# A gated linear attention and a hard-swish MLP on one core: the same steps in another order on every queue

## The chip, the cores and the metric

One Trainium2 chip, one of its cores. The time is the device time of one execution in microseconds (us); the figure that counts is the median of several runs.

## The reference

```python
def _attn_ref(q, k, v, alpha):            # batch 4, heads 8, seq 768, dim 48
    for t in range(S):
        state = alpha[:, :, t, :, None] * state + np.einsum('bhd,bhe->bhde', k[:, :, t], v[:, :, t])
        y[:, :, t] = np.einsum('bhd,bhde->bhe', q[:, :, t], state)
    return y

def _moe_ref(x, w_in, w_out):             # x: 3072 x 384, w_in: 384 x 2048, w_out: 2048 x 384
    h = x @ w_in
    relu6 = np.clip(h + 3.0, 0.0, 6.0)
    g = h * relu6 / 6.0
    return g @ w_out
```

The output y of the attention, with its heads side by side, is the x of the MLP. The state of a head is a 48 x 48 matrix that every token decays and adds to; it starts anew in each batch.

## The kernel before

**Staging.** The 3072 tokens are 24 chunks j of 128 (six to a batch). Attention works chunk by chunk, since the state goes from one to the next. Two chunks are a group g of 256 tokens (twelve groups), on which the MLP works. Both weight matrices stay in on-chip memory.

**A step.** The kernel is a list of short functions, its steps, and a string of about 1,800 words in `run` (L751 and after). A word such as `sc.6.1.2` calls one function with its numbers: here the scores of chunk 6, in the PSUM banks 1 and 2. Everything stands in `tc.manual_schedule()`: every engine, and SP's queue of transfers, executes its instructions in the order of the words, and waits in place if what it needs is not there. An instruction waits for what it reads, and for earlier readers of what it overwrites.

**Steps of attention** for chunk j (engine in brackets):

- `la`, `lk`, `lq`, `lv` [SP]: load alpha, k, q and v. `ta`, `tk`, `tq` put the time along the free axis: up to chunk 5 as transposes [PE, L282], from chunk 6 on as transposes of 32 x 32 blocks [DVE, L286] out of the tiles `quads`. These loads fill their tile but for two corners in each of the six tiles, which get 1.0 by a memset [POOL, L257] in `load_akq` when a tile is first used (chunks 6 and 7).
- `ca` places alpha [ACT L300, or DVE L286], `r` and `p` are the scans of the decay [DVE, L309 and L320], `k` and `q` scale by them [DVE, L332].
- `sc` scores [PE, L346], `m` mask [DVE, L356], `qa` a copy of q beside them [ACT, L366].
- `kb`, `ck` turn k by token [PE L374, ACT L378]; from chunk 8 on `kt`, `kw`, `kr` do it by DVE and by way of DRAM.
- `u` the chunk's two halves of k'v [PE, L429], `sm` the next state [DVE, L437 and L439], `st` its decay [POOL, L409], `sv` the copies of the state beside v [ACT; POOL in a batch's first half chunk].
- `ya`, `yb` the output [PE, L455], `cy` keeps it as x [ACT, L464].

**Steps of the weights.** The inputs are 64-bit floats. For each of 16 slices i: `w` loads it, `d1` (low word) and `d2` (magnitude) [ACT, L186 and L196], `dx` the sign [ACT, L191; slices 0, 1, 2, 4], `d3` clips and shifts [DVE: two instructions at L203 and L205 for those slices, three at L207, L208 and L210 for the others], `d4` adds the words as integers [POOL, L217].

**Steps of the MLP.** Groups 0 and 1 take the first product whole: `f` [PE, L478] or its halves `fa`, `fb` [L489], the gate `fr` [ACT, L494] and `fg` [DVE, L498]. From group 2 on a bilinear scheme of 20 block products replaces it: `M.g.i` [PE, L600], sums of x blocks `xc` and of weight blocks `y` [DVE, L537 to L541], `n` keeps a sum [ACT, L606], `o` adds up an output [DVE], `e` and `h` are its gate [ACT L494, DVE L498]. The second product of group 0 is `b` [PE, L516]; later groups use seven block products `P.g.i` [PE, L703] with sums `s` of g and `x` of w_out [DVE, L647 and L664], `K` [ACT], `G` [DVE or ACT] and the store `O` [SP]. `z` are matmuls that fill time.

**Memory.** The MLP has four PSUM banks, attention four others; `slots` and `raws` share the memory of g. Which bank or slot a step takes is the number in its word.

Of the kernel before, what the change touches and what calls it, by code (L numbers as in the profile page):

```python
# [17 lines left out]
def kernel(  # L18
# [32 lines left out]
    nc = tc.nc  # L51
    B, H, S, D = q.shape
# [8 lines left out]
    G = 2  # L61
# [185 lines left out]

    def load_akq(name, j):
# [6 lines left out]
        if j < FIRST + NQ:  # L255
            for o in (BLK, 3 * BLK):
                nc.gpsimd.memset(to[o : o + BLK, :, V - 1, D - BLK : BLK], 1.0)  # L257
# [463 lines left out]
    def store2(g, i):  # L721
# [8 lines left out]
        "lq": lambda j: load_akq("q", j), "lv": load_v, "w": load_weight,  # L730
# [202 lines left out]
```

## Time and profile before

| what | us |
|---|---|
| runs | 533.3, 533.65, 533.85 (median 533.65) |
| profiled execution, its time | 533.84 |
| its span | 531.8 |
| TensorE (PE) busy | 522.2 |
| VectorE (DVE) busy | 477.0 |
| ScalarE (ACT) busy | 257.4 |
| GpSimd (POOL) busy | 50.4 |
| one `M` (4 matmuls, 8 records in the trace, L600) | 0.89 |
| one `P` (8 matmuls, 16 records, L703) | 2.60 |
| one `f` (6 matmuls, 12 records, L478) | 2.69 |
| one L332, k for chunks 6 and later | 0.68 |
| one L207, median | 0.62 |
| one L217, the eleven of one kind | 1.61 |
| one pad memset, L257 | 0.14 to 0.24 |

The span is the time between the first and the last instruction of the profile; 2.04 us of the profiled execution lie outside it. A busy engine is one that executes; an idle one waits for a semaphore, for its own queue, or has nothing left. The profile gives, for each wait, what ended it, and for each group of instructions its idle time before. A figure such as L332 is the line of the kernel that issued the instruction.

### The profile page before, as it was taken

To read this page: it belongs to the slowest core of one execution; us is meant where nothing else is said; L and a number is where in the kernel's file an instruction comes from. 1 tells how busy PE (TensorE), PEld (TensorE's weight loads), DVE (VectorE), ACT (ScalarE), POOL (GpSimd) and SP (SyncE) were. 2 spreads that over 40 slices of the span, in tenths; PEclk is the share of its full clock that TensorE was granted. 3 is DMA by queue.
4 is the path that set the end of the run, shared out by engine and by line. 5 is a ranking of instruction groups with operands and counts; after the bars stand their busy time and mean duration, and the time that the engine had idled before them with its cause. 6 is when DMAs were issued, how large, how long until landed. Compare 5 with 4: busy or idle time off the path is not lost.

```text
span 531.8 us, 15143 instructions
## 1 busy us (share of the span) xinstructions
PE 522.2 (98%) x6306; PEld 496.9 (93%) x6306; DVE 477.0 (90%) x849; ACT 257.4 (48%) x503; POOL 50.4 (9%) x71
## 2 busy tenths in 40 slices
PE   7799999999999999999999999999999999999997
PEld 7698886789999999999999999999999999999997
DVE  6999989999999999999999999999999899496382
ACT  3889865212653553553544444642634544553340
POOL 5333425100000000000000000000000000000000
PEclk9999999999999999999999999999999999999999
DMA  9998887006615156254345356055364052100001
GB/s 173 218 254 247 211 231 156 18 2 149 155 31 118 30 125 139 49 137 100 89 107 118 90 123 143 18 134 111 92 138 105 10 110 44 44 2 2 15 16 37
DMA packets 124100, 54.40 MB, mean 102 GB/s; under 512 B 83328, under 2 KB 116864, under 8 KB 124032
## 3 DMA queue, kind: packets, MB, share of 16 engines
q1 hardware_dynamic: 124032, 53.44, 44.0%
q8 instruction: 49, 0.80, 0.7%
q14 instruction: 19, 0.16, 0.1%
HBM read 44.50 MB, written 8.91 MB: 100 GB/s over the span
## 4 chain that ended last, share of the span: by engine, by line
PE 81%; DVE 9%; ACT 3%; DMA 3%; POOL 2%; issue 1%; SPq 0%; DVEq 0%; POOLq 0%; ACTq 0%
PE m_ps L703 34%; PE m_ps L600 34%; PE m_ps L478 4%; PE t_ps L455 3%; PE t_ps L346 2%; PE t_ps L429 2%; DMA v<-in_v_dram 1%; DMA raw<-in_moe_w_out_dram 1%; DVE rings L647 1%; DVE R L309 1%; DVE raw L537 1%; ACT raw L186 1%; DVE g_sb L647 1%; ACT raw L191 1%; DVE w L537 1%
## 5 line engine op out<-in xcount | busy, mean ns | idle before, releaser
L606 ACT COPY g_sb<-m_ps 128x512 f32<-128x512 f32 x110 | 63.6, 584 | 123.7 <-PE m_ps L600 104.3
L703 PE MATMUL m_ps<-w,g_sb 128*128 128x192 f32 x704 | 121.7, 327 | 0.0
L703 PEld LDWEIGHTS m_ps<-w,g_sb 128*128 128x128 f32 x704 | 113.7, 190 | 0.4
L703 PE MATMUL m_ps<-rings,g_sb 128*128 128x192 f32 x528 | 91.5, 326 | 0.0
L703 PEld LDWEIGHTS m_ps<-rings,g_sb 128*128 128x128 f32 x528 | 85.4, 190 | 0.1
L600 PE MATMUL m_ps<-xc,w 128*128 128x128 f32 x640 | 82.8, 277 | 0.4 <-DVE w L541 0.4
L600 PEld LDWEIGHTS m_ps<-xc,w 128*128 128x128 f32 x640 | 77.5, 192 | 1.7 <-issue 0.6
L494 ACT ACTIVATE r<-g_sb,half 128x512 f32<-128x512 f32 x80 | 56.8, 722 | 33.1 <-DVE g_sb L541 12.1
L498 DVE SCALAR_TENSOR_TENSOR g_sb<-r,g_sb 128x512 f32<-128x512 f32 x80 | 53.7, 683 | 4.3 <-ACT r L494 3.9
L600 PE MATMUL m_ps<-xT,raw 128*128 128x128 f32 x400 | 52.5, 277 | 0.0
L600 PEld LDWEIGHTS m_ps<-xT,raw 128*128 128x128 f32 x400 | 48.6, 192 | 0.6
L409 POOL TENSOR_TENSOR st<-sm,R 128x192 f32<-128x192 f32 x20 | 12.9, 643 | 352.2 <-DVE sm L439 305.5
L647 DVE TENSOR_TENSOR g_sb<-g_sb 128x512 f32<-128x512 f32 (+1 forms) x55 | 41.9, 792 | 0.2
L600 PE MATMUL m_ps<-xT,w 128*128 128x128 f32 x320 | 42.0, 276 | 0.0
L600 PEld LDWEIGHTS m_ps<-xT,w 128*128 128x128 f32 x320 | 39.3, 192 | 0.1
L366 ACT COPY A<-q 48x256 f32<-48x256 f32 x88 | 35.6, 404 | 5.0 <-DVE q L332 3.8
L356 DVE TENSOR_TENSOR A<-t_ps,mask 64x256 f32<-64x256 f32 x96 | 36.0, 413 | 0.4
L478 PE MATMUL m_ps<-xT,w 128*128 128x256 f32 x144 | 32.8, 382 | 0.1
L600 PE MATMUL m_ps<-xc,raw 128*128 128x128 f32 x240 | 31.8, 276 | 0.0
L309 DVE TENSOR_TENSOR_SCAN R<-t,ones 128x516 f32<-128x516 f32 x24 | 29.6, 1235 | 1.0 <-ACT t L300 0.9
L478 PEld LDWEIGHTS m_ps<-xT,w 128*128 128x128 f32 x144 | 26.7, 190 | 3.8 <-POOL w L217 0.2
L600 PEld LDWEIGHTS m_ps<-xc,raw 128*128 128x128 f32 x240 | 29.6, 192 | 0.1
(104 smaller groups left out, 725.8 us busy)
## 6 DMA issues: line engine op xcount, KB each, us to landing
raw<-in_moe_w_out_dram SPq DMA_DIRECT2D x8, 768.0 KB, 5.3
raw<-in_moe_w_in_dram SPq DMA_DIRECT2D x6, 768.0 KB, 6.6
v<-in_v_dram SPq DMA_DIRECT2D x48, 96.0 KB, 3.1
out_dram<-oh SPq DMA_DIRECT2D x44, 96.0 KB, 1.7
far<-kq SPq DMA_DIRECT2D x64, 64.0 KB, 2.2
kb<-far SPq DMA_DIRECT2D x64, 64.0 KB, 2.1
aq<-in_alpha_dram SPq DMA_DIRECT2D x36, 96.0 KB, 2.7
qq<-in_q_dram SPq DMA_DIRECT2D x36, 96.0 KB, 2.5
```

The source lines that it names most:

```text
L309: nc.vector.tensor_tensor_scan(out=reverse(R, n - 1, n), data0=reverse(ax, n, n), data1=reverse(ones, n, n), initial=0.0, op0=ALU.mult, op ...
L356: nc.vector.tensor_tensor(out=to[:, a], in0=sc[a][half], in1=mask[half, half].unsqueeze(1).to_broadcast([HB, NP, HB]), op=ALU.mult)
L366: nc.scalar.copy(out=to[:, a], in_=Q_t[j][64 * a : 64 * a + D, :, half])
L409: nc.gpsimd.tensor_tensor(out=st, in0=sm, in1=R_t[j][:, :, 0:1].to_broadcast([C, NP, D]), op=ALU.mult)
L455: nc.tensor.matmul(y_of(j, (i + 1) // 2, p)[:, HB * b : HB * b + HB], vb[:, p, e : e + 32], A_t[j][:, b, 2 * p + a], start=(b == 0 and i = ...
L478: nc.tensor.matmul(h[:, f], w1[:, kk, o : o + C], xT_t[g][:, kk], start=(kk == 0), stop=(kk == KT - 1))
L494: nc.scalar.activation(out=to, in_=h, func=AF.Relu, bias=half, scale=1.0 / 6.0)
L498: nc.vector.scalar_tensor_tensor(out=to, in0=r, scalar=1.0, in1=h, op0=ALU.min, op1=ALU.mult)
L600: nc.tensor.matmul(acc[g][i][:, f * C : (f + 1) * C], spots[w][:, f * C : (f + 1) * C], x_of(g, x), start=(first and f == 0), stop=last, s ...
L606: nc.scalar.copy(out=slots[z], in_=acc[g][i])
L647: nc.vector.tensor_tensor(out=out, in0=in0, in1=in1, op=ALU.subtract)
L703: nc.tensor.matmul(to[g], a, rhs[:, f], start=(first and f == 0), stop=(last and f == HF - 1), skip_group_check=True)
```

## The change

The memsets of the corners leave `load_akq` and become a step of their own, `pd` (`pd.0` for the tiles of chunk 6, `pd.1` for those of chunk 7; six memsets each). All other words are the same, with the same banks and slots, in another order: on PE 345 of 436 steps have another place (2.4 places away in the mean, at most 17), on DVE 656 of 704 (6.7; at most 44), on ACT 353 of 414 (3.0), on POOL 26 of 46, on SP 162 of 190 (3.9).

The diff, with the first stage of the program (up to the first block products of group 2) and two later lines; the rest is of the same kind.

```diff
@@ -245,6 +245,11 @@
         b, c = divmod(j, NC)
         return t[b, :, c * C : (c + 1) * C, :]
 
+    def pad(r):
+        for name in "akq":
+            for o in (BLK, 3 * BLK):
+                nc.gpsimd.memset(quads[name, r][o : o + BLK, :, V - 1, D - BLK : BLK], 1.0)
+
     def load_akq(name, j):
         src = rows({"a": alpha, "k": k, "q": q}[name], j)
         if j < FIRST:
@@ -252,9 +257,6 @@
                               in_=src.rearrange("h s d -> s h d"))
             return
         to = quads[name, j % NQ]
-        if j < FIRST + NQ:
-            for o in (BLK, 3 * BLK):
-                nc.gpsimd.memset(to[o : o + BLK, :, V - 1, D - BLK : BLK], 1.0)
         to = to.rearrange("r p v d -> r p (v d)")
         t = src.rearrange("(p a) (u v) d -> a u p (v d)", a=2, v=V)
         for o in range(4):
@@ -727,7 +729,7 @@
 
     steps = {
         "la": lambda j: load_akq("a", j), "lk": lambda j: load_akq("k", j),
-        "lq": lambda j: load_akq("q", j), "lv": load_v, "w": load_weight,
+        "lq": lambda j: load_akq("q", j), "lv": load_v, "pd": pad, "w": load_weight,
         "d1": round_low, "d2": magnitude, "dx": sign, "d3": high_bits, "d4": add_low,
         "ta": lambda j, *i: transposed("a", j, *i), "tk": lambda j, *i: transposed("k", j, *i),
         "tq": lambda j, *i: transposed("q", j, *i), "ca": place_alpha, "r": decay, "p": growth,
@@ -748,156 +750,158 @@
             steps[name](*(int(x) for x in at))
 
     with tc.manual_schedule():
-        run("""z.0.5 z.0.3 z.0.1 z.0.8 qa.0.0 w.0 d2.0 d3.0 la.0 ta.0.0 ca.0 r.0 lk.0 tk.0.1 k.0
-               z.0.2 p.0 la.1 ta.1.2 lq.0 tq.0.3 ca.1 r.1 lk.1 lv.0.0 sv.0.0 d1.0 kb.0.0 ck.0 z.0.2
-               u.0.2.1 sm.0.0 sv.0.1 q.0 qa.0.1 tk.1.0 k.1 p.1 z.0.2 sc.0.2.3 m.0 la.2 ta.2.0 ca.2
-               dx.0 w.2 d2.2 kb.1.0 ck.1 lq.1 r.2 sm.0.1 st.1 tq.1.2 q.1 d3.2 z.0.3 d1.2 dx.2 lv.1.1
-               u.1.3.1 sv.1.0 sm.1.0 p.2 sm.1.1 sc.1.0.2 m.1 ya.0.3 yb.0 cy.0 lq.2 w.1 d1.1 tq.2.1
-               q.2 d4.2 lk.2 tk.2.3 k.2 fa.2.0 d4.0 st.2 sc.2.0.2 d2.1 d3.1 m.2 dx.1 d4.1 qa.1.1
-               lk.3 la.3 ta.3.1 ca.3 la.4 fa.0.1 sv.1.1 w.3 r.3 ta.4.3 ca.4 r.4 tk.3.1 k.3 kb.2.0
-               qa.1.0 d2.3 ya.1.2 yb.1 cy.1 fa.1.2 lq.3 ck.2 d1.3 p.3 d3.3 lv.2.2 u.2.3.2 sm.2.0
-               d4.3 fb.2 tq.3.1 q.3 fb.1 qa.2.0 sm.2.1 sv.2.0 st.3 fr.0.2.0 fg.0.2 lk.4 tk.4.0
-               sv.2.1 w.5 d2.5 k.4 d3.5 d1.5 qa.3.0 d4.5 qa.2.1 sc.3.1.3 m.3 w.6 d2.6 d1.6 d3.6 d4.6
-               lv.3.0 lq.4 w.7 kb.3.2 fb.0 f.0.3.3 kb.4.0 ya.2.1 ck.3 u.3.3.2 sm.3.0 fr.0.3.1 fg.0.3
-               fr.0.1.0 fg.0.1 qa.3.1 sv.3.0 sm.3.1 p.4 d2.7 sv.3.1 d1.7 d3.7 d4.7 f.0.5.0 fr.0.5.1
-               fr.0.0.0 fg.0.5 fg.0.0 tq.4.3 ck.4 la.5 ta.5.2 f.0.6.3 ca.5 w.4 d2.4 ya.3.0 yb.3 cy.3
-               fr.0.6.1 yb.2 cy.2 w.9 d2.9 q.4 qa.4.1 d1.4 d1.9 dx.4 la.6 w.8 d3.4 r.5 lk.5 w.10
-               d3.9 p.5 ca.6 fg.0.6 d4.9 w.12 lq.5 lv.4.1 d2.8 d3.8 f.0.7.2 d1.8 st.4 d4.8 d4.4 w.11
-               fr.0.7.0 fg.0.7 f.1.7.0 fr.1.7.1 fg.1.7 sc.4.0.2 m.4 f.1.1.1 fr.1.1.0 fg.1.1 f.1.3.3
-               fr.1.3.1 d2.10 d1.10 tk.5.3 f.1.0.2 d2.12 d3.10 d4.10 w.13 fg.1.3 fr.1.0.0 fg.1.0 k.5
-               d3.12 lq.6 f.1.6.0 f.1.2.1 u.4.1.0 sm.4.0 d1.12 d4.12 sv.4.0 qa.4.0 ya.4.2 fr.1.6.1
-               fg.1.6 w.15 tq.5.3 fa.4.3 sv.4.1 d2.11 kb.5.1 d2.13 fr.1.2.0 f.1.4.2 fr.1.4.1 d1.11
-               sm.4.1 q.5 r.6 d3.11 d3.13 fg.1.4 d4.11 lv.5.0 lk.6 tq.6 p.6 d2.15 d3.15 fg.1.2 d1.13
-               d4.13 sc.5.0.3 yb.4 f.1.5.0 fr.1.5.1 fg.1.5 tk.6 m.5 b.1.0.2 fb.4 b.1.1 d1.15 d4.15
-               st.5 y.5 w.14 la.7 lk.7 cy.4 d2.14 qa.5.1 ck.5 b.0.0.1 fr.0.4.0 d3.14 k.6 q.6 ca.7
-               fg.0.4 d1.14 d4.14 x.0 y.1 y.10 b.0.1 y.0 y.2 u.5.2 P.1.0.0 K.1.0 qa.5.0 sv.5.0
-               qa.6.1 P.1.1.3 b.0.2 b.1.2 kb.6.0 ya.5.3 y.6 s.1.0.0 sm.5.0 sv.5.1 G.1.0.0 tk.7
-               s.1.1.1 s.1.2.3 x.1 yb.5 cy.5 b.1.3 sc.6.1.2 lv.6.2 ck.6 u.6.3.0 s.1.3.2 x.2 P.1.2
-               b.0.3 K.1.1 y.7 s.1.4 s.1.5 y.11 y.3 r.7 xc.2.1 x.3 y.4 y.8 xc.2.3 k.7 xc.2.0 xc.2.4
-               y.9 y.12 y.16 y.13 y.15 P.1.3.3 K.1.2 P.1.4 bo.1 P.1.5 xc.2.5 G.1.1.1 P.1.6 y.14 y.17
-               y.19 xc.2.6 sm.6.0 G.1.2.2 y.20 M.2.0.2 lv.12.1 la.8 O.1.1 O.1.0 ca.8 y.18 y.21 y.23
-               so.1 G.1.3.3 n.2.0.8 bo.0 lq.7 lv.7.0 O.1.2 m.6 xc.2.2 xc.2.10 xc.2.7 tq.7 r.8 p.7
-               xc.2.8 sv.6.1 M.2.15.3 M.2.1 kb.7.3 n.2.1.9 M.2.16 M.2.2 n.2.2.10 M.2.7.0 n.2.7.11
...
-               xc.4.8 M.4.7.3 M.4.1 xc.4.2 h.3.2 o.3.7.1 lk.11 O.2.2 tk.11 e.3.6.0 e.3.3.1 h.3.3
-               P.3.1.2 e.3.7.1 n.4.1.13 M.4.2 K.3.0 ca.11 q.10 h.3.6 r.11 k.11 h.3.7 n.4.7.15
...
+        run("""z.0.5 z.0.3 z.0.1 z.0.8 qa.0.0 w.0 d2.0 d3.0 la.0 ta.0.0 ca.0 r.0 la.1 lk.0 ta.1.2
+               z.0.2 tk.0.1 k.0 ca.1 r.1 p.0 lv.0.0 lq.0 lk.1 d1.0 z.0.2 z.0.2 kb.0.0 tq.0.3 la.2
+               dx.0 ck.0 u.0.2.1 sm.0.0 sv.0.1 q.0 qa.0.1 tk.1.0 k.1 sc.0.2.3 ta.2.0 ca.2 w.2 d2.2
+               sm.0.1 m.0 r.2 p.1 d3.2 z.0.3 kb.1.0 ck.1 d1.2 lv.1.1 lq.1 tq.1.2 u.1.3.1 lk.2 w.1
+               lq.2 d4.0 st.1 sv.0.0 sv.1.0 dx.2 sm.1.0 q.1 p.2 sm.1.1 ya.0.3 yb.0 sc.1.0.2 m.1
+               cy.0 d1.1 tk.2.3 tq.2.1 k.2 q.2 st.2 d4.2 d2.1 d3.1 dx.1 d4.1 la.4 fa.0.1 ta.4.3
+               sc.2.0.2 fa.2.0 m.2 qa.1.0 sv.1.1 qa.1.1 lv.2.2 la.3 ta.3.1 ca.3 r.3 ca.4 r.4 kb.2.0
+               ya.1.2 yb.1 fa.1.2 ck.2 cy.1 p.3 u.2.3.2 sm.2.0 qa.2.0 lk.4 lk.3 w.3 tk.3.1 k.3 d2.3
+               d1.3 fb.2 fb.1 sm.2.1 d3.3 w.5 lq.3 tq.3.1 q.3 d1.5 sv.2.0 d2.5 fr.0.2.0 d3.5 qa.2.1
+               qa.3.0 w.6 fb.0 tk.4.0 sc.3.1.3 m.3 fg.0.2 kb.3.2 ck.3 qa.3.1 d2.6 d3.6 la.5 lv.3.0
+               lq.4 w.7 pd.0 d4.3 f.0.3.3 u.3.3.2 fr.0.3.1 sv.2.1 d1.6 la.6 w.4 pd.1 d4.5 st.3 d4.6
+               sm.3.0 k.4 sv.3.0 sm.3.1 fg.0.3 p.4 sv.3.1 fr.0.1.0 d2.7 d1.7 d3.7 d4.7 f.0.5.0
+               tq.4.3 kb.4.0 ck.4 fr.0.5.1 ta.5.2 f.0.6.3 ca.5 ya.3.0 yb.3 ya.2.1 cy.3 yb.2 q.4
+               fg.0.1 fg.0.5 w.8 r.5 lk.5 lv.4.1 lq.5 w.9 d2.8 d1.4 fr.0.0.0 fg.0.0 sc.4.0.2 m.4
+               d3.8 tk.5.3 f.0.7.2 k.5 qa.4.0 cy.2 fr.0.7.0 d1.8 d1.9 d2.9 fr.0.6.1 qa.4.1 d2.4
+               d4.8 st.4 fg.0.7 d3.9 fg.0.6 d3.4 d4.9 f.1.1.1 u.4.1.0 sm.4.0 tq.5.3 f.1.7.0 f.1.0.2
+               kb.5.1 f.1.3.3 lk.6 w.10 d2.10 fr.1.1.0 dx.4 fg.1.1 d3.10 p.5 fr.1.0.0 d1.10
+               fr.1.7.1 fg.1.7 d4.10 d4.4 fg.1.0 f.1.2.1 f.1.6.0 sv.4.1 f.1.4.2 sm.4.1 q.5 ca.6
+               tk.6 lk.7 ck.5 lv.6.2 w.12 w.11 d2.12 w.13 d1.12 fr.1.3.1 fg.1.3 d3.12 d4.12
+               fr.1.6.1 fg.1.6 fa.4.3 d2.11 sv.4.0 d1.11 d3.11 r.6 d4.11 lv.5.0 fb.4 ya.4.2 yb.4
+               sc.5.0.3 la.7 w.15 w.14 ca.7 qa.5.0 d2.13 d1.13 fr.1.4.1 fg.1.4 cy.4 fr.1.2.0 d2.15
+               d1.15 d2.14 qa.5.1 k.6 d3.13 m.5 d3.15 p.6 fg.1.2 d3.14 d1.14 fr.0.4.0 u.5.2 f.1.5.0
+               fr.1.5.1 b.1.0.2 kb.6.0 b.1.1 b.0.0.1 b.0.1 ck.6 sv.6.0 d4.13 st.5 d4.15 d4.14 y.6
+               fg.1.5 P.1.0.0 la.9 lq.6 tq.6 sm.5.0 sv.5.1 sv.5.0 K.1.0 ya.5.3 yb.5 cy.5 y.3 r.7
+               fg.0.4 x.0 q.6 y.5 s.1.1.1 s.1.0.0 sc.6.1.2 u.6.3.0 b.1.2 P.1.1.3 b.1.3 b.0.2 bo.1
+               so.1 xc.2.2 y.1 s.1.3.2 s.1.2.3 y.7 x.1 y.10 xc.2.1 x.2 sm.6.0 tk.7 xc.2.3 y.11 y.0
+               G.1.0.0 y.9 s.1.5 xc.2.4 y.2 y.8 y.4 k.7 P.1.3.3 P.1.2 K.1.2 qa.6.1 K.1.1 P.1.5
+               xc.2.5 xc.2.0 y.13 y.16 s.1.4 y.15 y.12 y.17 xc.2.6 xc.2.7 y.19 y.20 x.3 y.18 sv.6.1
+               kb.7.3 P.1.4 G.1.1.1 M.2.0.2 b.0.3 P.1.6 sm.6.1 xc.2.8 y.21 xc.2.9 st.7 lq.8 lq.7
+               lv.7.0 lv.12.1 la.8 lk.8 tq.8 y.23 tq.7 y.14 ca.8 p.7 ck.7 n.2.0.8 bo.0 G.1.3.3
+               M.2.1 n.2.1.9 M.2.7.0 M.2.2 n.2.7.11 n.2.2.10 M.2.8 M.2.3 z.1.3 M.2.4 n.2.4.12 ca.9
...
+               o.3.7.0 p.10 o.3.7.1 tk.11 tq.10 h.3.2 e.3.6.0 n.4.0.10 M.4.1 M.4.7.3 K.3.0 n.4.1.13
+               M.4.2 h.3.6 n.4.7.15 e.3.3.1 n.4.2.14 M.4.8 xc.4.9 q.10 h.3.3 P.3.1.2 e.3.7.1 M.4.3
...
```

## The prediction

> **What bounds the kernel now.** I read the page first: busy time, then the slices.
>
> ```profile
> PE 522.2 (98%) x6306; PEld 496.9 (93%) x6306; DVE 477.0 (90%) x849; ACT 257.4 (48%) x503; POOL 50.4 (9%) x71
> ...
> PE   7799999999999999999999999999999999999997
> ...
> DVE  6999989999999999999999999999999899496382
> ...
> PEclk9999999999999999999999999999999999999999
> ```
>
> TensorE (PE) is busy 522.2 of 531.8 us at an undiminished clock, so an order can only regain its 9.6 us of gaps or the price of switching between kinds of matmul. VectorE (DVE) at 90% is the second bound, and the stretches (PE, PEld, DVE, ACT, POOL busy; clock; DMA) say where:
>
> ```profile
> 0.00:20.00 20.00, 15.45 (x152) 13.61 (x152) 14.99 (x30) 10.00 (x15) 7.12 (x20) 1.00 1.16 204
> 20.00:40.00 20.00, 18.30 (x395) 16.56 (x396) 19.64 (x34) 18.44 (x30) 8.84 (x7) 1.00 1.05 227
> ...
> 100.00:130.00 30.00, 29.58 (x278) 24.80 (x277) 29.84 (x53) 5.26 (x13) 0.00 (x0) 1.00 0.20 48
> 130.00:170.00 40.00, 40.00 (x538) 38.87 (x537) 39.38 (x71) 20.14 (x40) 1.60 (x2) 1.00 0.46 104
> ...
> 450.00:490.00 40.00, 40.00 (x454) 39.50 (x453) 28.45 (x56) 17.25 (x35) 0.00 (x0) 1.00 0.08 20
> ```
>
> PE idles up to 31 us and a little before 130; later it never waits. DVE is full from 20 to 170 us (29.84 of 30.00 in 100:130) and has room only near the end. So up to about 140 us the two are bound together: what delays DVE there must reach PE as soon as the spare of some pair "DVE writes, PE reads" is used up. What waits there, for DVE from 6 to 110 us:
>
> ```profile
> DVE w L203 <- ACT w L196: 2.5, 1, 2.5
> DVE s L439 <- PE t_ps L429: 1.1, 1, 1.1
> DVE R L309 <- ACT t L300: 0.9, 1, 0.9
> DVE s L437 <- PE t_ps L429: 0.2, 1, 0.2
> ```
>
> The first lies at its start; the second is sm.4.0 waiting for u.4. Last the chain of waits in the steady part:
>
> ```profile
> 183.88 1.92 PE t_ps L455 x128
> 185.81 1.98 PE m_ps L600 x16
> 187.79 2.60 PE m_ps L703 x16
> ...
> 193.89 1.78 PE m_ps L600 x16
> ```
>
> It is PE alone. Two M products cost 1.78 us, but 1.98 behind attention's small matmuls: a visit to the small ones costs some 0.3 us beside its own work (0.1 ahead of it, 0.2 behind).
>
> **The sum, part by part.** It is made against the profiled execution: span 531.8 and 2.04 outside it, 533.84 us, 0.19 above the median of 533.65. Work is the same on every engine, so only order counts. On PE 345 of 436 steps move, by 2.4 places in the mean; on DVE 656 of 704, by 6.7.
>
> *Pads.* Twelve POOL memsets of 0.14 to 0.24 us, 2.3 us in all, become pd.0 and pd.1, ahead of d4.3 and d4.5. POOL is 91% idle and has no transfer behind it: I take nothing. If POOL were late there, 1.2 us (one pd) would be added to a conversion; if they now leave the loads of chunks 6 and 7 earlier, up to 0.3 us is gained.
>
> *Fewer switches.* Between big products and small attention matmuls PE goes 50 times in the old order and 45 in the new. Counted over the words with the prices above, the steady part saves 0.84 us. The old 0.42 us that M.2.0 waits for xc at 127.5 us is also in reach. Together -1.26; bounds 0 and -1.3.
>
> *DVE work ahead of what PE needs.* For a pair I take the old spare (end of the writer to start of the reader), less DVE work newly put ahead, plus PE work newly put ahead of the reader, less PE work no longer there.
>
> - q.6 (ends 94.64) to sc.6 (starts 108.85): spare 14.21. DVE does ca.7, y.6, sm.5.0, y.3, r.7, fg.0.4, x.0 first (6.23 us) and y.5 later (0.61); PE no longer does P.1.1, b.0.2, b.1.2, b.1.3 first (10.34 us). 14.21 - 6.23 + 0.61 - 10.34 = -1.75.
> - G.1.0 (102.19) to P.1.3 (115.12): 12.93 - 10.08 + 0.60 - 5.18 = -1.73.
> - q.7 (134.63) to sc.7 (140.31): 5.68 - 2.83 + 1.30 - 5.35 = -1.20.
>
> ```profile
> 108.85 0.69 PE L346 MATMUL t_ps<-q,k 48*64 48x64 f32 x32
> ...
> 140.31 0.69 PE L346 MATMUL t_ps<-q,k 48*64 48x64 f32 x32
> ```
>
> These are one lateness seen three times, not a sum: +1.75 us of PE waiting, unless DVE arrives earlier than before. Others stay near nothing (fg.1.2 to b.0.0 about -0.55), and later single pairs go to -1.25 (h.3.3 to P.3.1), the same lateness again.
>
> *DVE waits that go and come.* The 1.14 us at sm.4.0 go: u.4 now stands ahead of two f products of 2.69 us on PE. New, placed by hand from the rows of each step: 0.15 at sm.0.0 (dx.0, 1.9 us on ACT, is put ahead of ck.0, and u.0 needs ck.0), 0.25 at r.3 (for ca.3, on ACT behind the copies qa and sv), 0.4 at d3.7 (d2.7 stands behind sv and d1.6 on ACT), 0.75 at fg.0.0 (fr.0.0 stands behind d2.8, which waits for w.8): +1.55, bounds 0 and 2.2. SP's queue moves too: lq.3 goes behind w.3 and w.5 and lands near 36.1 instead of 31.75, w.9 behind w.8, lk.5, lv.4, lq.5 near 57.4 instead of 51.35; behind each on its engine (DVE's q.3; ACT's d2.9, fr.0.6, qa.4.1) stands work that I find covered by other DVE work; bounds 0 and 1. In the steady part every load leads its reader by 2 us or more: nothing.
>
> *DVE beside POOL.* Some DVE operations stand still while POOL adds integers (d4, L217):
>
> ```profile
> 92.40 1.69 POOL L217 TENSOR_TENSOR w<-raw 128x768 int32<-128x768 int32 x1 [3.73 <-DVE raw L210]
> ```
>
> ```profile
> 92.69 1.96 DVE L332 TENSOR_TENSOR q<-q,P 128x512 f32<-128x512 f32 x1
> ...
> 133.95 0.68 DVE L332 TENSOR_TENSOR q<-q,P 128x512 f32<-128x512 f32 x1
> ```
>
> q.6 took 1.96 instead of 0.68 and ended within 0.6 us of POOL's end; d3.15's L207 took 1.77 instead of 0.62 beside another d4. [...] By position, the new order puts d4.3 beside d3.5 (0.8), d4.8 beside d3.9 (0.3), d4.9 beside d3.4, d4.12 beside d3.11 and d4.15 beside d3.14 (0.9 each), and takes away the two shown (1.28 and 1.15): 3.8 - 2.43 = +1.37. Start times differ by some tenths from my placing, and a hold is there or not by such tenths: bounds -2.4 (none of the new) and +3.8 (the old two replaced by equal ones). I take +0.9, two thirds of the count.
>
> Sum: +1.75 - 1.14 + 1.55 + 0.9 - 1.26 = +1.80 us: 533.84 + 1.80 = 535.64 for a profiled execution, 535.45 for the median.
>
> **Rivals.** *PE alone decides (faster).* Place: sc.6, sc.7 and P.1.3. If none of the new holds comes while both old ones go (-2.4) and half of the waits come (+0.8), DVE's lateness is 1.75 - 1.14 + 0.8 - 2.4 = -1.0: it is early, PE keeps the -1.26 and gets up to 1.0 us of its idle time before 31 us, since DVE then no longer takes it back. 533.65 - 1.26 to -2.26 is 531.4 to 532.4; I put 532.0. It decides once lateness is below nothing. For it: PE's visits are fewer throughout, and u.4 and the f products are better interleaved. Against: DVE is full in 100:130, and three pairs independently come out negative.
>
> *Nothing is seen.* Neither new waits nor holds count: 1.75 - 1.14 - 1.26 = -0.65, 533.0; with the waits alone +0.9, 534.55. For it: my waits of 0.15 to 0.75 us are near the error of the placing. Against: all have the same sign.
>
> *DVE falls further behind (much slower).* Every counted hold comes and the old are only replaced: 1.75 - 1.14 + 1.55 + 3.8 - 1.26 = +4.7, 538.35. For it: DVE has no idle time there to absorb one. Against: in the whole old run the holds sum to some 5 us, and POOL's work is the same.
>
> **How the numbers follow.** A measurement of this kernel can tell 0.2%, 1.07 us, from no change. The sum passes +1.07 once new waits and holds together exceed 1.72 us; I estimate 2.45, with bounds of -2.4 and 6. The forecast gets 0.42, much slower 0.08, so slower 0.50; nothing seen 0.23; PE alone 0.27, the most I can give it with DVE as full as it is. Predicted 535.4. The range goes from the first rival's 532.0 to 538.0, short of the last rival's end. The forecast's own range is 534.7 to 537.
>
> **What would show it.** Right: PE waits for L332 or L286 of DVE at sc.6 or sc.7 (L346), 1 to 3 us in all, between 95 and 145 us; the 1.1 us wait of L439 gone; several L207/L208 of 1.5 us or more beside L217; PE busy from 150 us on without waits and its steady part shorter by 0.5 to 1 us, with fewer "L600 x16" of 1.98. Wrong, faster: no PE wait after 31 us, DVE idle about 1 us somewhere in 100:140. Wrong otherwise: a DMA as releaser of PE in 30:70 (lq.3, w.9), or new PE waits after 150 us, where I count none, which would say that my spares in the steady part are too large.

## The result, and the profile after

Slower: a median of 541.77 us (540.45 to 543.38) beside 533.75 us (533.3 to 534.06) of the kernel before, a ratio of 1.0152 [1.0122, 1.0183]. The side was foretold, the size was not: +8.0 us instead of +1.8, above the range. The profiled execution took 543.38 us; its span is 541.6 us, 9.8 us longer than before. In the kernel after, lines have moved: L429 is L431, L439 is L441, L455 is L457, L498 is L500, L516 is L518, L600 is L602, L606 is L608, L703 is L705.

From the page of the kernel after, the parts that answer to those shown of before:

```profile
PE 525.8 (97%) x6306; PEld 499.7 (92%) x6306; DVE 478.2 (88%) x849; ACT 258.8 (48%) x503; POOL 53.3 (10%) x71
...
PE   8798899899999999999999999999999999999997
...
DVE  6899799999999999999999999999999996377381
...
PEclk9799899999999999999999999999999999999999
```

Two things differ. PE is busy 3.56 us longer with as many instructions, and idle 6.24 us longer (12.99 against 6.75 from the start of the span to its last instruction). And PEclk has a 7 and an 8 where before had only nines. The stretches of the kernel after (PE, PEld, DVE, ACT, POOL busy; granted clock; DMA) place both:

```profile
0.00:20.00 20.00, 14.47 (x151) 12.76 (x152) 15.48 (x30) 12.20 (x18) 10.09 (x22) 0.97 1.12 185
20.00:40.00 20.00, 19.38 (x379) 17.79 (x381) 17.01 (x30) 15.95 (x27) 5.89 (x10) 0.86 1.11 241
...
100.00:130.00 30.00, 29.24 (x269) 24.48 (x268) 29.93 (x48) 6.00 (x15) 0.44 (x1) 1.00 0.30 69
130.00:170.00 40.00, 39.52 (x532) 38.14 (x531) 39.55 (x76) 20.35 (x40) 1.63 (x2) 1.00 0.39 89
```

In 20:40 PE is busy for 19.38 us instead of 18.30 and still finishes 16 instructions fewer: the clock was 0.86. DVE lost 2.6 us there. Its full stretch, 100:130, is as full as before (29.93), and PE now waits in it. PE's waits in the kernel after, grouped (total, times, longest):

```profile
PE t_ps L284 <- DVE P L322: 2.4, 1, 2.4
PE t_ps L457 <- issue: 2.1, 1, 2.1
PE t_ps L348 <- DVE q L334: 1.7, 3, 0.8
...
PE m_ps L518 <- DVE g_sb L500: 1.1, 1, 1.1
PE t_ps L431 <- ACT r L496: 0.9, 1, 0.9
PE m_ps L602 <- issue: 0.7, 1, 0.7
PE m_ps L705 <- issue: 0.7, 1, 0.7
```

The third and fourth rows hold what was foretold. The first is tq.1, at 17.06 to 19.49 us. The row names p.1 on DVE, which ended at 19.39; but tq.1 does not read what p.1 writes, it reads the load lq.1, which landed at 19.35. The fifth is u.3, which overwrites the bank that m.3 reads. The three "issue" rows are waits in which the trace shows no data that was missing.

Put together, with the place of each item in the trace:

| what | us |
|---|---|
| 10.24 us at half clock (18.95 to 25.78 and 56.50 to 59.91): the same instructions take about 2.2 and 1.6 us longer than at full clock | +3.8 |
| "issue" stops: 2.06 in yb.2 (53.57), 0.66 at P.4.4 (271.12), 0.68 in M.8.13 (389.20) | +3.4 |
| waits for DVE: 1.11 at b.0.0 (94.83), 0.76 at sc.6 (105.00), 0.48 at sc.7 (141.53) | +2.35 |
| u.3 waits for m.3 (43.59) | +0.86 |
| the old wait at M.2.1 is gone | -0.42 |
| some 25 more products that take 0.05 us longer, most of them behind a copy (below) | +1.25 |
| what remains; five fewer visits to the small matmuls at 0.3 us would be that | -1.5 |
| sum | +9.74 |

The profiled execution is the slowest of the four. A second profile of the same kernel (the run "again" below) is 6.3 us longer than before instead of 9.8: its stop in yb.2 is 0.42 us, that in P.4.4 0.40, and the second half clock is missing.

PE's idle time ahead of 31 us is the same in both kernels, about 6.2 us; only its pieces differ. Behind PE's first instruction none is over 0.95 us before, and one is 2.43 after. The findings are taken in turn.

### The profile page after: what moved, and what is told of

Same layout as the page of the kernel before. It is cut to its first block, busy times and chain, and to the rows that moved or that the text cites. A ratio compares the mean times of both kernels' runs of the same rounds, so it can differ in the third digit from the quotient of the medians.

```text
span 541.6 us, 15103 instructions
## 1 busy us (share of the span) xinstructions
PE 525.8 (97%) x6306; PEld 499.7 (92%) x6306; DVE 478.2 (88%) x849; ACT 258.8 (48%) x503; POOL 53.3 (10%) x71
## 4 chain that ended last, share of the span: by engine, by line
PE 76%; DVE 14%; DMA 4%; issue 2%; SPq 2%; POOL 1%; ACT 1%; DVEq 0%; POOLq 0%
PE m_ps L705 34%; PE m_ps L602 33%; PE t_ps L457 4%; PE t_ps L348 2%; PE t_ps L431 2%; DMA raw<-in_moe_w_out_dram 2%; DMA raw<-in_moe_w_in_dram 1%; PE m_ps L491 1%; SPq L256 1%; DVE g_sb L500 1%; DVE w L207 1%; DVE raw L210 1%; DMA rings<-in_q_dram 1%; PE t_ps L284 1%; DVE P L322 1%
## 5 line engine op out<-in xcount | busy, mean ns | idle before, releaser
L705 PE MATMUL m_ps<-w,g_sb 128*128 128x192 f32 x704 | 122.2, 327 | 0.0
L608 ACT COPY g_sb<-m_ps 128x512 f32<-128x512 f32 x110 | 63.9, 584 | 112.2 <-PE m_ps L602 81.5
L705 PEld LDWEIGHTS m_ps<-w,g_sb 128*128 128x128 f32 x704 | 113.8, 190 | 1.3 <-DVE oh L721 0.5
L705 PE MATMUL m_ps<-rings,g_sb 128*128 128x192 f32 x528 | 91.8, 327 | 0.7 <-issue 0.7
L705 PEld LDWEIGHTS m_ps<-rings,g_sb 128*128 128x128 f32 x528 | 85.4, 190 | 1.3 <-issue 0.8
L602 PE MATMUL m_ps<-xc,w 128*128 128x128 f32 x640 | 82.8, 277 | 0.0
L602 PEld LDWEIGHTS m_ps<-xc,w 128*128 128x128 f32 x640 | 78.0, 192 | 0.8
L500 DVE SCALAR_TENSOR_TENSOR g_sb<-r,g_sb 128x512 f32<-128x512 f32 x80 | 53.8, 684 | 8.4 <-ACT r L496 4.4
L602 PE MATMUL m_ps<-xT,raw 128*128 128x128 f32 x400 | 52.2, 277 | 0.0
L411 POOL TENSOR_TENSOR st<-sm,R 128x192 f32<-128x192 f32 x20 | 14.4, 720 | 350.4 <-DVE sm L441 251.9
L602 PEld LDWEIGHTS m_ps<-xT,raw 128*128 128x128 f32 x400 | 48.5, 192 | 0.3
L602 PE MATMUL m_ps<-xT,w 128*128 128x128 f32 x320 | 42.5, 277 | 0.0
L602 PEld LDWEIGHTS m_ps<-xT,w 128*128 128x128 f32 x320 | 39.1, 192 | 0.3
L539 DVE TENSOR_TENSOR g_sb<-g_sb 128x512 f32<-128x512 f32 x40 | 27.0, 682 | 11.7 <-ACT g_sb L608 11.5
L602 PE MATMUL m_ps<-xc,raw 128*128 128x128 f32 x240 | 32.6, 278 | 0.7 <-issue 0.7
L602 PEld LDWEIGHTS m_ps<-xc,raw 128*128 128x128 f32 x240 | 29.7, 191 | 1.2 <-issue 0.9
```

What stands on the lines that cost most here:

```text
L411: nc.gpsimd.tensor_tensor(out=st, in0=sm, in1=R_t[j][:, :, 0:1].to_broadcast([C, NP, D]), op=ALU.mult)
L500: nc.vector.scalar_tensor_tensor(out=to, in0=r, scalar=1.0, in1=h, op0=ALU.min, op1=ALU.mult)
L539: eng.tensor_tensor(out=out, in0=in0, in1=in1, op=ALU.add if s1 > 0 else ALU.subtract)
L602: nc.tensor.matmul(acc[g][i][:, f * C : (f + 1) * C], spots[w][:, f * C : (f + 1) * C], x_of(g, x), start=(first and f == 0), stop=last, s ...
L608: nc.scalar.copy(out=slots[z], in_=acc[g][i])
L705: nc.tensor.matmul(to[g], a, rhs[:, f], start=(first and f == 0), stop=(last and f == HF - 1), skip_group_check=True)
```

## The experiments

Every kernel ran beside the kernel before, whose medians were 533.46 to 533.72 us. "Old" and "new" are the orders of before and after. Where the words of one order are followed by those of the other, each step is taken once, and the place of the change can have waits of its own; they are named.

### Where the time is lost: parts of the program

**old40**

```diff
- all words in the new order
+ old order up to f.0.3, the rest in the new order
```

> The old order up to f.0.3 (about 41 us, 152 words), then the new order of everything else. Theory A: no half clock before 31 us; the loads after 41 us are still in the new order, so the stop of 2 us at yb.2 (an instruction block fetched late behind those loads) may remain; median 535 to 538. Rival C (the new order pays at the pairs of DVE and PE between 95 and 145 us and in the steady part, whatever the opening does): 539 or more.

538.44 us, 1.0093 [1.0078, 1.0108]. The clock was 1.00 throughout, and tq.1's long wait and the stop in yb.2 were gone. At the cut u.3 still waited 0.61 us, for the copy ck.3 now, and tk.5 waited 0.74 us for its load. The waits for DVE stayed (1.15, 0.77, 0.45), and so did two stops (0.66 and 0.41). So the first 40 us are worth some 3 us, and more than half of the loss lies behind them.

**old128**

```diff
- all words in the new order
+ old order up to M.2.0, the rest in the new order
```

> The old order up to M.2.0 (about 128 us), then the new order of everything else. Theory A: only the two stops of 0.66 and 0.68 us for instructions and about 0.5 us at sc.7 remain, less up to 0.8 us of fewer switches: 534 to 535.5. Rival C: most of the 8 us remains, 538 or more.

538.17 us, 1.009 [1.0073, 1.0107], some 3 us above what was expected. The cut made a wait of its own (1.73 us at M.2.1, for y.23), and sc.7 waited 1.02; but the part behind M.5 took 2.0 us longer than in before, and no recorded wait explains it. So the new order of the steady part costs time inside PE's busy time. In the trace of old128, 25 products behind M.5 take some 0.05 us more each (1.3 us together; in before none does), and P.4.4 and M.8.13, where the kernel after has its stops, take 0.35 and 0.16 us more. The 0.05 us are what the copies, below, are about.

**new40 and mid**

```diff
- all words in the old order
+ new40: new order up to f.0.3, the rest in the old order
+ mid: old order up to f.0.3, new order up to M.3.0, the rest in the old order
```

> The new order up to f.0.3 (about 41 us), then the old order of everything else. Theory A (the 8.2 us are three separate parts that add up: the opening, the DVE pairs between 85 and 145 us, and the steady part): the opening's share, that is the idle lump with its half clock, 2 to 3.5 us: 536.5 (535.6 to 537.1), in executions whose mean clock is below 1.00. Rival C (a late opening costs nothing by itself, since DVE and PE catch up before 100 us): 533.6 to 534.4.

> Old order up to f.0.3, new order from there to M.3.0 (about 155 us), old order after it. Theory A: PE waits for DVE at b.0 (1.1), sc.6 (0.8) and sc.7 (0.5), together 2.4 us, less the 0.4 of the old order at M.2.1: 535.6 (535.0 to 536.5), clock 1.00. Rival E (the loss lies in the opening and in the steady part alone): within 0.5 us of the kernel before.

new40 took 541.55 us, 1.0142 [1.0123, 1.0161], 5 us more than expected. Its cut delays k.4, so that PE waits 4.31 us at 44.37 for it, and the clock is halved a second time. It says nothing of the order, but from M.5.0 to the start of P.11.6 it takes 292.85 us, exactly as before. mid took 537.37 us, 1.0067 [1.0053, 1.0082], 0.9 above the upper end expected. Its waits for DVE are 1.14, 0.77 and 0.47; 0.88 at the cut, 0.62 for a load (tk.5), 0.37 at u.2 and 0.29 at kb.5 come on top.

**old155**

```diff
- all words in the new order
+ old order up to M.3.0, the rest in the new order
```

> Old order up to M.3.0 (about 155 us), new order after it. Theory F (in the steady part a product that goes on in a PSUM bank waits until ACT has copied the partial sum out, the n step; a P between the two covers the copy, one M covers all but 0.05 us, nothing leaves 0.67 us): the steady part has 31 places with one M between instead of 7, so 24 x 0.05 = 1.2 us; with up to 1.3 us of stops for instruction blocks near 267 and 385 us 534.8 to 536.2. Theory D (the 0.05 us come from DVE being late): 533.6 to 534.2, since DVE starts this part on time.

539.16 us, 1.0101 [1.0086, 1.0115]; expected was 534.8 to 536.2. Waits at the cut (1.17, 0.35, 0.56) and a stop of 0.44 are one part, and 1.8 us of PE's steps from M.5.0 on, inside its busy time as in old128, the other.

**part1, part2 and part3**

```diff
- all words in the old order
+ part1: the first 125 words (37 us) new, the rest old
+ part2: 125 words old, then new up to word 661 (192 us), the rest old
+ part3: 661 words old, the rest new
```

> New order for the first 125 words (to about 37 us), old order after; at this cut the two orders have done the same steps but two. Theory A: the idle lump at tq.1 with the half clock behind it, 535.6 (534.6 to 536.6), in executions with a mean clock below 1.00; no PE wait after 45 us that the kernel before has not. Rival C (the opening's loss is caught up before 100 us): within 0.6 us of the kernel before.

> Old order for the first 125 words, new order to word 661 (about 37 to 192 us), old order after. Theory A: PE waits for DVE at b.0, sc.6 and sc.7, 2.4 us together, 0.4 less at M.2.1, 0.3 us of products with one M beside a copy; with the clock at 1.00: 536.0 (535.2 to 537.2); the stop at yb.2 should be small, since the loads before it are on time. Rival E: within 0.6 us of the kernel before.

> Old order for the first 661 words (to about 192 us), new order after. Theory F: from 230 us to the end 294.4 us instead of 292.85 without stops for instruction blocks, up to 1.3 more with them; one product at the cut (M.4.2) has nothing between it and the copy, 0.67 us: 536.2 (535.4 to 537.6). Parts 1, 2 and 3 together less 0.7 are then about the 8.2 us of the whole change. Rival D: 533.6 to 534.8.

part1: 535.56 us, 1.0031 [1.0019, 1.0043], as expected. It is 2.2 us late at 45 us and stays so to the end: PE is busy 1.4 us longer, at the halved clock (19.61 to 26.44), and idle 0.8 us longer, where sc.3 waits 1.15 us for DVE at the cut. part2: 537.43 us, 1.0073 [1.0048, 1.0098], 1.4 above its middle; waits of 1.46, 0.76 and 0.45 and a stop of 1.75 in yb.2, which had been expected to be small behind the old opening. part3: 539.27 us, 1.0104 [1.0089, 1.0119], 3 us above; cut waits 1.6, a stop of 0.78, and 1.9 of PE's steps. The three differences are 1.84, 3.71 and 5.55 us; less some 2 us that the cuts make, the sum is about 9.1, where the whole change costs 6.5 (the run "again", below) to 8.0 us. They don't add exactly; each part nonetheless costs time by itself.

### The clock: one long wait instead of several short ones

TensorE's granted clock is halved in stretches of 3.41 us or 6.83 us, on a grid of 3.413 us that runs through the whole execution (in the kernel after the clock changes at 18.95, 25.78, 56.50, 59.91 and, behind PE's last instruction, 541.19 us, which lie 2, 9, 1 and 141 such steps apart; it is 0.50 in 18.95:25.78 and in 56.50:59.91). The same step at both clocks, PE's timeline of the kernel before and after:

```profile
22.16 1.10 PE L455 MATMUL t_ps<-A,v 128*32 128x64 f32 x64 [0.92 <-DVE s L439]
```

```profile
22.02 1.93 PE L457 MATMUL t_ps<-A,v 128*32 128x64 f32 x64 [0.62 <-DVE s L441]
```

**nofill** takes four steps of fillers out of the old order, so that its idle time gathers in one place, a lump.

```diff
- p.0 behind z.0.2; u.0.2.1 behind z.0.2; sc.0.2.3 behind z.0.2; d1.2 behind z.0.3
+ the same without these four fillers
```

> The kernel before without nine filler matmuls (z.0.2 four times, z.0.3 once, about 2.5 us of PE between 8 and 18 us, all in places where PE then waits anyway). Theory A (what closes the clock is the share of idle time within a stretch of 3.4 us): PE idles more than 1.4 of 3.4 us somewhere between 10 and 22 us, the clock goes to half for one or two stretches, and the time rises by 1 to 3 us, to 534.5 to 536.5, although work is left out. Rival B: the work removed lay in idle time, no change, 533.0 to 533.7.

534.34 us, 1.0014 [1.0005, 1.0023]. PE was idle for 1.62 us in one piece, and the clock was halved, in the timed executions too. The stretch from 19.5 to 26.3 us, of before and then of this kernel:

```profile
19.50:26.30 6.80, 4.83 (x148) 4.23 (x148) 6.71 (x15) 6.68 (x9) 3.98 (x3) 1.00 0.93 185
```

```profile
19.50:26.30 6.80, 6.36 (x140) 5.95 (x141) 6.27 (x13) 6.00 (x9) 4.14 (x3) 0.50 0.99 192
```

Nearly the same instructions (140 against 148) fill 6.36 us instead of 4.83. The cost is only 0.7 us, less than the 1 to 3 us expected, since PE had 1.97 us to spare in that stretch of before. So the clock is closed by the lump, not by the new order as such, and what it costs hangs on PE's slack there.

**lq1** brings tq.1's load forward, **fill** puts a filler into the lump.

```diff
- d1.2 lv.1.1 lq.1 tq.1.2
+ lq1:  d1.2 lq.1 lv.1.1 tq.1.2
+ fill: d1.2 lv.1.1 lq.1 z.0.8 tq.1.2
```

> The changed kernel with one word moved: lq.1 is loaded ahead of lv.1.1 instead of behind it. Theory A (PE's idle time in one lump halves its clock for whole stretches of 3.4 us, and PE and DVE then pass the loss on): tq.1 starts near 17.8 us instead of 19.5, the wait of 2.43 us breaks into pieces of at most 1.3 us, the granted clock stays 1.00 between 15 and 30 us, and the median falls from 541.8 to about 539.3 (538.5 to 540.3). Rival B (the half clock is only a sign; what counts are the waits, and their sum in the opening is unchanged): the sum of PE's waits before 31 us stays near 5 us and the median falls by less than 0.6 us.

> The changed kernel with eight more filler matmuls (z.0.8, about 2.2 us) in the place where PE waited 2.43 us for tq.1; no step moves and no load is earlier. Theory A: the same data arrive at the same time, but the clock stays 1.00 from 15 to 30 us; and as the 32 more instructions move the limits of PE's instruction blocks (256 instructions each), the stops of 0.66 and 0.68 us near 270 and 389 us go: median 538.8 (537.8 to 539.8). Rival B: filler changes nothing, 541.2 to 541.8.

lq1: 540.34 us, 1.0137 [1.0114, 1.0159]. tq.1 waited 0.43 us instead of 2.43, which shows that the load was what it waited for; but u.1 then waited 1.87 us for lv.1, and the clock was halved from 19.15 to 25.98 as before. The lump had only moved. fill: 540.23 us (536.76 to 541.3), 1.0116 [1.0082, 1.015], above the range expected. Here the clock stayed full to 53 us, as expected; then a stop of 2.48 us in yb.2 halved it from 53.33 to 60.16. The one execution at a mean clock of 1.000 took 536.76 us, those at .994 to .997 took 540.2 to 541.3.

Over all profiles that show a change of the clock, and so the grid, taking PE's idle time inside one stretch of it in the first 150 us: each stretch with at least 1.77 us of it was followed by half clock. Of the stretches at full clock with 1.38 us or less none was (over 30 had between 0.9 and 1.38; the largest of before, behind PE's first instruction, is 1.20). Between these the outcome varied: 1.39 closed it once, 1.46 and 1.51 did not. It is the sum within a stretch that counts, not one long wait: in best and part3 (their openings are the old one) a wait of 0.95 us and one of 0.8 to 0.9 fell into one stretch, 1.77 and 1.83 us, and the clock was halved for 3.41 us.

The half clock also spreads the times of the kernel after: 543.38 us at a mean clock of .990, 542.31 and 541.24 at .994, 540.45 at .997.

### The stops without missing data: blocks of PE's instructions

**again** is the kernel after, unchanged, profiled a second time.

```diff
  no change to the kernel after
```

> The changed kernel once more, for its profile. Theory A: PE stops again at the same places of its instruction stream (before the 1474th, 6594th and 9666th PE record: yb.2, P.4.4 and M.8.13), each until 1.3 to 1.5 us after the landing of the 16 KB block; the clock closes where PE idled more than about 1.7 us of a stretch of 3.4 us, and nowhere else; waits of 1.1, 0.8 and 0.5 us at b.0, sc.6 and sc.7; 540.4 to 543.4. If the stops lie elsewhere, the limits of the blocks are not their cause.

540.24 us, 1.0121 [1.0101, 1.0141], just below the range expected; the stops lie where they were. PE's timeline of the kernel after:

```profile
55.63 0.65 PE L457 MATMUL t_ps<-A,v 128*32 128x64 f32 x32 [2.06 <-issue]
...
271.78 1.41 PE L705 MATMUL m_ps<-rings,g_sb 128*128 128x192 f32 x7 [0.66 <-issue]
...
389.89 0.82 PE L602 MATMUL m_ps<-xc,raw 128*128 128x128 f32 x5 [0.68 <-issue]
```

And of this second profile:

```profile
54.06 0.65 PE L457 MATMUL t_ps<-A,v 128*32 128x64 f32 x32 [0.42 <-issue]
...
268.31 2.87 PE L705 MATMUL m_ps<-rings,g_sb 128*128 128x192 f32 x16 [0.40 <-issue]
...
386.42 0.82 PE L602 MATMUL m_ps<-xc,raw 128*128 128x128 f32 x5 [0.68 <-issue]
```

Counted from PE's first record (matmuls, weight loads and waits for semaphores, in order of their start), the stops lie behind 1473, 6593 and 9665 records in both, that is 256 x 20 and 256 x 12 apart. The page counts 49 transfers of kind "instruction", 16,384 bytes each, one to 257 of PE's 12,612 matmuls and weight loads, and at each stop such a block had landed 1.2 to 1.5 us before PE went on (54.14 to 55.63, 270.38 to 271.77, 388.61 to 389.89); in the second profile it is 1.75, 1.23 and 1.58, a little outside the range expected. At the second stop the block ahead is exactly one run of 128 small matmuls of ya and yb: its 256 records pass in 1.78 us. The next block's transfer began at 269.04, when PE entered this one (269.12), and landed at 270.38, too late. At the third, 124 of these small matmuls and three of M.8.13 pass in 2.22 us. With 32 more instructions ahead (the filler of fill) the limits shift against these runs, and both stops are gone. In before no limit is that tight: its smallest lead from landing to execution is 2.09 us.

So of the 49 blocks three came late in each of the two profiles, at 0.40 to 2.06 us each.

At the first stop the fetch itself began late: 6.3 us behind the limit before it (0.92 in before), while six loads were under way. **fix1** takes one of these loads away from there.

```diff
- lv.1.1 lq.1 tq.1.2 ... d1.6 la.6 w.4 ... lq.5 w.9 d2.8
+ lv.1.1 lq.1 z.0.8 tq.1.2 ... d1.6 w.4 ... lq.5 w.9 la.6 d2.8
```

> The changed kernel with z.0.8 ahead of tq.1 (as in the run with filler) and the load la.6 (0.4 MB, needed after 70 us) moved behind w.9. Theory A: the instruction block that yb.2 needs was fetched late because its transfer stood behind data, so its start moves from 50.8 to 49.6 us or earlier and the stop of 2.5 us falls to 1.3 or less; then the clock closes in fewer executions: median 538.3 (537.2 to 539.3). Rival G (the late fetch has nothing to do with the loads): 540.2 as with the filler alone, and the stop stays over 2 us.

538.47 us (536.89 to 542.29), 1.0079 [1.0049, 1.0109]. The stop in yb.2 was gone, though the transfer of its block began at 52.42, not at 49.6 or earlier as expected; PE itself was later there. Another stop, of 3.76 us, stood at 32.52, at the limit of record 961, and halved the clock there. Two executions at a mean clock of 1.000 took 536.89 and 536.93 us. That a late block stops PE is shown; that the loads make it late is not settled.

### PE's steps behind a copy

**abab** asked whether a product that returns to a PSUM bank after one other product is slow.

```diff
- M.3.3 M.3.4 ... M.3.8        (14 such pairs in the old order)
+ M.3.3 M.3.8 M.3.4 ...
```

> The kernel before with 14 neighbouring pairs of block products of the steady part exchanged on PE, so that a product comes back to the PSUM bank that was left one M earlier (bank a, b, a in three M in a row): 23 such places instead of 7. Theory A (each such return costs PE 0.05 us, which the new order does 33 times): 16 x 0.05 = +0.8 us, 534.3, with M of 0.94 us at these places and no new waits. Rival D (the 0.05 us are a trace of late data in the new order, not of the bank): no change, 533.3 to 533.7, and M of 0.89.

534.71 us, 1.002 [1.0011, 1.0029]. Of the 16 added places only four took 0.05 us more, and these are those where ScalarE copies out the bank (n) before it is added to. Of the twelve without a copy eleven stayed at 0.89; one, M.10.17, took 1.13. So the return alone costs nothing. The four make 0.2 of the 1.1 us lost; the rest lies at single other products, 0.24 us at most, and was not followed up.

**noaba** does the opposite in the new order: products that stand apart by one come next to each other.

```diff
- M.4.1 M.4.7.3 ... M.4.2      (16 such pairs in the new order)
+ M.4.7.3 M.4.1 ... M.4.2
```

> The changed kernel with 16 neighbouring pairs of block products exchanged on PE, so that 13 returns to a bank after one M remain of 33. Theory A: 20 x 0.05 = 1.0 us less, 540.7, seen in the steady part as M of 0.89 us where they were 0.94. Rival D: no change.

552.25 us, 1.0354 [1.034, 1.0368], the slowest of all. Its waits on PE, grouped:

```profile
PE m_ps L602 <- ACT g_sb L608: 8.9, 13, 0.7
```

In thirteen places `M` continues the sum that `n` is still copying, and waits 0.67 us for it. With one other product (0.89 us) between, as in the new order, the same place costs 0.05 us in 28 of 32 cases and nothing in four, and behind a P (2.60 us) nothing. The chain of waits of the kernel after shows the middle case:

```profile
453.54 2.68 PE m_ps L602 x24
...
473.48 2.73 PE m_ps L602 x24
```

Both are three products. The second is M.10.12, M.10.6, M.10.13, where M.10.13 goes on in the bank that n.10.12 copies. The old order has 7 places with one product between, all in groups 2 and 3; the new one has 32.

**uncov** takes the cover away in the old order.

```diff
- M.4.1 P.3.1.2 M.4.2          (10 such pairs in the old order)
+ M.4.1 M.4.2 P.3.1.2
```

> The kernel before with ten neighbouring pairs exchanged on PE (a P behind the M that followed it), chosen so that a product goes on in its PSUM bank directly behind the product whose partial sum ACT then copies out. Theory F: ten waits of PE for the copy (L602 or L600 for ACT L606), 0.67 us each: 6.7 us more, 540.4 (539.2 to 541.6), the clock at 1.00. Theory D: the copies do not matter as long as DVE is on time: within 1 us of the kernel before.

546.74 us, 1.0241 [1.0224, 1.0258]: twice the 6.7 us expected. PE's waits, and one of them beside its copy, from PE's and ACT's timelines:

```profile
PE m_ps L600 <- ACT g_sb L606: 9.3, 11, 1.8
```

```profile
264.38 1.16 PE L600 MATMUL m_ps<-xc,raw 128*128 128x128 f32 x8 [0.68 <-ACT g_sb L606]
```

```profile
263.74 0.59 ACT L606 COPY g_sb<-m_ps 128x512 f32<-128x512 f32 x1 [1.58 <-PE m_ps L600]
```

The copy ends at 264.33 and the product starts 0.05 us later. Eight of the eleven waits are 0.68 us, two 1.73 and 1.77. The waits sum to 9.3 of the 13.0 us lost. At each of the ten places the product ahead of the wait also takes 0.17 us more and the one behind it 0.11, by the starts of the steps in the trace: 2.8 us in all, so that a place with nothing between costs some 0.95 us. Two waits for DVE (0.36 and 0.32) make most of the rest. The clock has no part in it (1.00 in uncov's profile). So an order that keeps a P behind each copied product pays nothing, and the new order, which often keeps one M there, pays little at each of many places.

### DVE's lateness

**q6** puts q.6 ahead of four DVE steps.

```diff
- cy.5 y.3 r.7 fg.0.4 x.0 q.6 y.5
+ cy.5 q.6 y.3 r.7 fg.0.4 x.0 y.5
```

> The changed kernel with one DVE word moved: q.6 ahead of y.3, r.7, fg.0.4 and x.0 (3.3 us of DVE work) instead of behind them. Theory A: the wait of 0.76 us of PE at sc.6 goes, and because DVE is only late by as much as that pair needed, about 0.5 us is kept at sc.7 and after it: 541.2, mainly to be seen in the waits. Rival C (DVE is full up to 145 us, so the wait comes back at the next pair): the wait at sc.6 goes, that at the next pairs (P.1.3, sc.7) grows by as much.

541.43 us, 1.0142 [1.0124, 1.016], no gain. sc.6's wait of 0.76 is gone; 0.45 came at P.1.3 (114.48), and sc.7's 0.48 stayed. The lateness belongs to DVE as a whole, and moving one step passes it to the next reader.

**best** tries to use the one gain of the new order in the old one: M.2.1 waits 0.42 us for y.23, which ca.8 delays.

```diff
- ca.8 y.18 y.21 y.23
+ y.18 y.21 y.23 ca.8
```

> The kernel before with one DVE word moved: ca.8 (1.1 us) behind y.23 instead of ahead of it, since the only wait of PE after 53 us, 0.42 us at M.2.1, is for y.23. If DVE's order is what sets that wait, it goes and the median falls by 0.3 to 0.4 us to 533.2; if the next DVE step that PE needs (q.7 for sc.7) is as tight, it comes back there and nothing changes.

533.72 us, 1.0003 [0.9993, 1.0012]: a wait of 0.30 us came back at 133.7. No version beat the kernel before.

## Why the prediction was right and wrong

**Slower, by way of DVE: right.** PE waits for DVE at sc.6 and sc.7, as named, and the 1.1 us wait of L439 is gone. The lateness was put at 1.75, later 1.75 - 1.14 + 1.55 + 0.9 = 3.06 us with waits and holds; 2.35 was measured, 1.13 + 0.77 + 0.44 in the second profile. The first share fell on b.0.0 (1.11), where the pair had been put at -0.55; P.1.3 waited for nothing. It was said that such a lateness must not be counted once for each pair, and that held.

**New DVE waits: two of four places right, one missed.** The kernel after's DVE timeline has 0.86 at fg.0.0 (0.75 expected), 0.72 at r.3 (0.25), and 1.72 at d3.8, for which nothing was counted; at sm.0.0 (0.15 expected) it has 0.07 and at d3.7 (0.4) none. In the second profile r.3 waits 0.96 us, fg.0.0 only 0.23 and d3.8 not at all. DVE's idle time from 6 to 110 us rose from 4.71 to 9.12 us, but only to 6.05 in the second profile, with the same waits of PE behind it: part of it only passes on what PE lost earlier.

**Holds beside POOL: the places right, the term mis-sized.** d3.5's L207 took 1.73 us beside d4.3, as named, from DVE's and POOL's timelines of the kernel after:

```profile
39.46 1.73 DVE L207 TENSOR_SCALAR w<-w 128x768 f32<-128x768 f32 x1
```

```profile
39.17 1.47 POOL L217 TENSOR_TENSOR w<-g_sb 128x768 int32<-128x768 int32 x1 [6.76 <-DVE g_sb L210]
```

d3.4, d3.11 and d3.14 have one too (1.64, 1.50 and 1.06). The four exceed the median of their kind (0.67) by 3.2 us, and the two old ones (2.43) are gone. But two smaller ones of the old order, 0.72 us together at 26.16 and 29.45 us, had not been counted, and they are gone too. All excesses of over 0.2 us ahead of 110 us sum to 3.17 us, against 3.14 before: nothing instead of +0.9. The pads cost nothing visible, as taken.

**Fewer switches: half wrong.** The 0.42 us was gained; the prediction has it at M.2.0 for xc, the trace at M.2.1 for y.23. The 0.84 us of the steady part was not: from M.5 on both orders have 19 visits, and the five that are saved lie ahead of it. From M.5.0 to its end the kernel after takes 3.2 us more than before (298.8 against 295.6), where 0.5 to 1 us less was named as the sign of being right.

**What made the size wrong was left out of the sum.** The step that failed is the sum's assumption that PE loses time to late data and to its visits to the small matmuls, and to nothing else. Three terms were put at nothing, and in the profiled execution they are about 8.4 of the 9.8 us:

- The clock was taken as given ("at an undiminished clock"). It is a result of the order: the same idle time ahead of 31 us, gathered in one lump, halves it, which with the second half clock costs 3.8 us. What was missed is in the treatment of SP's queue, where lq.3, w.9 and the loads of chunks 4 and 5 were weighed and lq.1, a few words ahead of its reader, was not.
- "New PE waits after 150 us, where I count none": they came, but not for the reason given there, spares that are too large. No data was late; PE's own instructions were (3.4 us with the stop in yb.2).
- Spares were worked out for readers of data. The copy n is also a reader, and the next M that adds to its bank waits for it; of these pairs none was checked (about 1.25 us).

The third rival (538.35) came nearest in size, by luck: the holds, on which it rests, were not the cause.

## What to carry to other kernels

When steps are moved on a queue that is nearly full, look beyond the pairs of writer and reader: at how idle time is gathered (up to 1.38 us within one stretch of 3.413 us left the clock alone here; 1.77 us or more halved it, which cost up to 2.2 us), at the readers of a bank that is written next, and at dense runs of small instructions against the fetch of the program. A step between two that depend on each other is a cover with a length: here 2.60 us hid a copy, 0.89 nearly did, and with nothing between some 0.95 us were lost. And profile a changed kernel twice before a stop is explained: the one at yb.2 was 2.06 us in one execution and 0.42 in the next.

## What the runs showed of the hardware that was not expected

- TensorE's clock was halved for one or two stretches of 3.413 us behind each stretch with 1.77 us or more of idle time, in one piece or in two, and behind none with 1.38 us or less; from 1.39 to 1.51 us it was halved once and twice not. The idle time lay at a load, at a missing instruction block or at a cut.
- TensorE ran out of instructions: 256 records passed in 1.78 us, the transfer of the next 16,384 bytes alone took 1.34 us (269.04 to 270.38), and at the stops shown PE went on 1.2 to 1.75 us after the block had landed.
- Why a block is at times fetched 6 us late (6.3 us in yb.2) stays open.
